# One decode step of attention and a gated feed-forward: larger K, V and query-weight tiles, queries up front, V by pairs of rows, feed-forward over four quadrants

## The chip, the cores and the metric

The kernel runs on 1 core of one Trainium2 chip. The metric is the device time of one execution in microseconds; three runs of the kernel before gave 1093.95, 1096.56 and 1097.2 us.

## The reference

A single token `x` (640 numbers) passes through attention over a cache of 8192 keys and values in each of 32 heads of 192, and then through a gated feed-forward of width 1536. Everything is float32.

```
xn = layernorm(x)
q = xn @ wq                              # wq: 640 x 6144 = 32 heads of 192
for each head: p = softmax(q . K / sqrt(192));  o = p @ V      # K, V: 8192 x 192
h = x + concat(o) @ wo                   # wo: 6144 x 640
hn = layernorm(h)
out = h + (relu(hn @ W_gate) * (hn @ W_up)) @ W_down           # 640 x 1536 twice, 1536 x 640
```

K and V are 402.7 MB of the 445.9 MB that have to be read from HBM. Each element is used once.

## The kernel before

**Loads.** Each head's K and V come in four chunks of 2048 positions. A chunk is one DMA into a tile of 128 partitions by 16 positions (`R = 16`, L35): each partition receives one row of 16 x 192 x 4 = 12,288 bytes that lie together in HBM, 1.57 MB in all. The pool `kv` has 12 such tiles (L55). All loads are issued by SyncE (SP) in program order: K of head h+1 and V of head h by turns (L232 to L238); before the first head of a pair the query weights of the next pair (`load_wq`, L77: 5 rows of 1,536 bytes per partition), before the second the pair's output weights (`load_wo`, L82: one row of 7,680 bytes per partition). An SP instruction whose buffer isn't free holds up all loads behind it. The kernel's loads use eight completion semaphores by turns, so that an issue also waits until the load eight places ahead of it has landed.

**Queries.** `project_q` (L137) makes the queries of two heads, spread to all partitions, in five 128x384 matmuls.

**Scores.** For each chunk VectorE multiplies K in place by the query (L146) and sums 10 of the 16 positions (L147); ScalarE sums the other 6 (L149). A softmax over the 64 x 128 scores follows (L155 to L170): a maximum on VectorE, TensorE to bring it to one partition and back, the exponential on ScalarE, TensorE and VectorE for the sum's reciprocal.

**Values.** For each position row TensorE takes one column of `p` as weights and 192 columns of V, and adds into one partition of `po` (L189): 64 matmuls per head, each recorded as two instructions. In the last two heads VectorE weighs half of the rows (L184, L186). Every two heads the output is turned to columns (L200, L202) and multiplied by the output weights into `acc` (L209), one partition and two banks.

**The last pair and the feed-forward.** The output weights of heads 30 and 31 are loaded as two tiles of 96 partitions (L228) in the two buffers of the tag `wo_t`; the second is issued between loads of V of head 30 and K of head 31. The layer norm of h works on one partition (L297 to L316). The feed-forward takes blocks of 512 columns (rows of 2,048 bytes; `W_down` in rows of 2,560 bytes), and VectorE weighs most slices (L332, L375), TensorE the others, all on one output partition.

Of the kernel before, what the change touches and what calls it, by code (L numbers as in the profile page):

```python
# [15 lines left out]
def kernel(  # L16
# [62 lines left out]

    def load_wo(g):  # L80
        t = wts.tile([P, GJ, D], F32, name="wo_t")
        nc.sync.dma_start(t, wo[g * GW:(g + 1) * GW, :].rearrange("(p j) n -> p j n", p=P))  # L82
        return t

    def load_kv(src, h, c, parts=1):
        t = kv.tile([P, R, DH], F32, name="kv_t")
        v = src[h, c * P * R:(c + 1) * P * R, :].rearrange("(p r) d -> p r d", p=P)
        n = R // parts
        for i in range(parts):
            nc.sync.dma_start(t[:, i * n:(i + 1) * n, :], v[:, i * n:(i + 1) * n, :])  # L90
# [38 lines left out]
    halves = [slice(0, DHALF), slice(DHALF, D)]
    acc = [ps_a.tile([1, DHALF], F32, name=f"acc{i}") for i in range(2)]  # L130
    for i in range(2):
        nc.tensor.matmul(acc[i], ones[0:1, 0:1], xrow[:, halves[i]], start=True, stop=False)

    def project_q(wq_t):
        q = ps_q.tile([P, GW], F32, name="q")
        for j in range(DJ):
            nc.tensor.matmul(q, xn[:, j:j + 1].to_broadcast([P, P]), wq_t[:, j, :],  # L137
                             start=(j == 0), stop=(j == DJ - 1))
        return q

    def scores_of(q, h, kts):
        sc = small.tile([P, NS], F32, name="sc")
        hh = h % GRP
        qb = q[:, hh * DH:(hh + 1) * DH]
        for c, kt in enumerate(kts):
            nc.vector.tensor_mul(kt, kt, qb[:, None, :].to_broadcast([P, R, DH]))  # L146
            nc.vector.reduce_sum(sc[:, c * R:(c + 1) * R - NA], kt[:, :R - NA, :], axis=AX.X)  # L147
# [4 lines left out]

    def softmax_of(sc):
# [16 lines left out]
        nc.vector.reciprocal(rl, pl[0:1, 0:1])  # L170
# [2 lines left out]
    def values_of(p, rl, vts, o, shared):
        """o = p @ V / l; with shared, VectorE weighs and adds some of the rows."""
        po = ps_o.tile([1, DH], F32, name="po")
        va = {}
        for c, vt in enumerate(vts):
            for r in range(R):
                i = c * R + r
                if shared and r % 2:  # L180
                    a = (r // 2) % 2
                    if a not in va:
                        va[a] = row.tile([P, DH], F32, name=f"va{a}")
                        nc.vector.tensor_scalar_mul(va[a], vt[:, r, :], p[:, i:i + 1])  # L184
                    else:
                        nc.vector.scalar_tensor_tensor(va[a], vt[:, r, :], p[:, i:i + 1], va[a],  # L186
                                                       op0=ALU.mult, op1=ALU.add)
                else:
                    nc.tensor.matmul(po, p[:, i:i + 1], vt[:, r, :], start=(i == 0),  # L189
                                     stop=(i == NS - 1))  # L190
        for a in va:
            nc.tensor.matmul(po, ones[:, 0:1], va[a], start=False, stop=(a == len(va) - 1))
        nc.scalar.activation(o, po, AF.Copy, scale=rl)  # L193

    def to_columns(src, n, np_, name):
        """src [1, n * np_] as columns [np_, n]; the row's element is p * n + j."""
        pt = ps_s.tile([P, 512], F32, name="ps_small")
        v = src.rearrange("o (p j) -> o p j", j=n)
        for j in range(n):
            nc.tensor.matmul(pt[0:np_, j:j + 1], v[:, :, j], ones[0:1, 0:1], start=True, stop=True)  # L200
# [1 line left out]
        nc.vector.tensor_copy(t, pt[0:np_, 0:n])  # L202
        return t

    def output_of(o, wo_t, n, np_, last):
        oT = to_columns(o, n, np_, "oT")
        for i in range(2):
            for j in range(n):
                mm = nc.tensor.matmul(acc[i], oT[:, j:j + 1], wo_t[:, j, halves[i]],  # L209
                                      start=False, stop=(last and j == n - 1))  # L210
# [224 lines left out]
```

## Time and profile before

| | |
|---|---|
| runs, us | 1093.95, 1096.56, 1097.2 (median 1096.56) |
| span of the profiled execution, us | 1093.9 |
| instructions | 12264 |
| busy: TensorE, its weight loads | 912.3 us (83%), 427.0 us (39%) |
| busy: VectorE, ScalarE | 767.2 us (70%), 322.4 us (29%) |
| granted TensorE clock, mean | 0.930 |
| read from HBM | 445.91 MB, 408 GB/s over the span |

The profiled execution's span is the lowest of the three times to within 0.1 us. In the profile's lines `128x3072 f32<-...` is output and input as partitions x elements; `x128` counts instructions, then come busy microseconds, mean nanoseconds of one, and idle time before them with what ended it. `SPq` and `ACTq` are the issue streams of SP and ScalarE, `PEld` the weight loads of TensorE.

### The profile page before, as it was taken

To read this page: it belongs to the slowest core of one execution; us is meant where nothing else is said; L and a number is where in the kernel's file an instruction comes from. 1 tells how busy PE (TensorE), PEld (TensorE's weight loads), DVE (VectorE), ACT (ScalarE), POOL (GpSimd) and SP (SyncE) were. 2 spreads that over 40 slices of the span, in tenths; PEclk is the share of its full clock that TensorE was granted. 3 is DMA by queue.
4 is the path that set the end of the run, shared out by engine and by line. 5 is a ranking of instruction groups with operands and counts; after the bars stand their busy time and mean duration, and the time that the engine had idled before them with its cause. 6 is when DMAs were issued, how large, how long until landed. Compare 5 with 4: busy or idle time off the path is not lost.

```text
span 1093.9 us, 12264 instructions
## 1 busy us (share of the span) xinstructions
PE 912.3 (83%) x4698; PEld 427.0 (39%) x4699; DVE 767.2 (70%) x487; ACT 322.4 (29%) x1683; POOL 1.2 (0%) x7
## 2 busy tenths in 40 slices
PE   4599888797988979788897979789797888977598
PEld 2244444343434434343443434334343433433242
DVE  5877767776676776767687766768667677764956
ACT  2423323323222332223232322323223223231220
POOL 0000000000000000000000000000000000000000
PEclk7799999998989989899998999999999999988799
DMA  9999999999999999999999999999999999996994
GB/s 373 425 427 418 425 421 424 420 424 425 422 424 420 425 421 425 425 421 424 420 425 420 424 425 420 425 419 425 422 422 425 421 423 421 425 406 211 414 396 154
DMA packets 55629, 446.70 MB, mean 408 GB/s; under 512 B 4946, under 2 KB 15186, under 8 KB 22932
## 3 DMA queue, kind: packets, MB, share of 16 engines
q1 hardware_dynamic: 55426, 445.93, 98.1%
q8 instruction: 36, 0.59, 0.2%
q14 instruction: 21, 0.17, 0.0%
q10 hardware_dynamic: 146, 0.01, 0.0%
HBM read 445.91 MB, written 0.00 MB: 408 GB/s over the span
## 4 chain that ended last, share of the span: by engine, by line
DMA 74%; PE 11%; DVE 7%; SPq 5%; ACT 2%; issue 1%; ACTq 0%; DVEq 0%
DMA kv_t<-in_A_v_cache_dram 36%; DMA kv_t<-in_A_k_cache_dram 33%; PE po L189 7%; SPq L90 5%; DVE kv_t L146 4%; DMA wq_t<-in_A_wq_dram 3%; DMA wo_t<-in_A_wo_dram 3%; DVE sc L147 1%; ACT kv_t L149 1%; PE acc L209 1%; PE prq L343 1%; PE q L137 1%; DVE va L186 0%; DVE da L375 0%; PE prq L344 0%
## 5 line engine op out<-in xcount | busy, mean ns | idle before, releaser
L189 PE MATMUL po<-kv_t,p 128*1 128x192 f32 x3968 | 716.2, 344 | 129.0 <-DMA kv_t<-in_A_v_cache_dram 129.0
L189 PEld LDWEIGHTS po<-kv_t,p 128*1 128x1 f32 x3968 | 340.2, 88 | 501.9 <-DMA kv_t<-in_A_v_cache_dram 157.3
L146 DVE TENSOR_TENSOR kv_t<-kv_t,q 128x3072 f32<-128x3072 f32 x128 | 428.7, 3350 | 115.8 <-DMA kv_t<-in_A_k_cache_dram 108.7
L149 ACT ACTIVATE kv_t<-kv_t 128x192 f32<-128x192 f32 x768 | 267.6, 349 | 569.4 <-DVE kv_t L146 569.4
L147 DVE TENSOR_REDUCE sc<-kv_t 128x10 f32<-128x1920 f32 x128 | 275.5, 2153 | 3.8
L149 ACT ACTIVATION_READ_ACCUMULATOR kv_t<-kv_t 128x1 f32 x768 | 143.4, 187 | 0.0
L159 DVE TENSOR_REDUCE m<-ps_small 1x1 f32<-1x128 f32 x32 | 8.9, 278 | 124.7 <-PE ps_small L157 124.7
L137 PE MATMUL q<-wq_t,xn 128*128 128x384 f32 x160 | 71.0, 552 | 10.6 <-DMA wq_t<-in_A_wq_dram 10.0
L193 ACT ACTIVATE o<-po,rl 1x192 f32<-1x192 f32 x32 | 13.2, 412 | 143.0 <-PE po L189 127.3
L209 PE MATMUL acc<-wo_t,oT 128*1 128x320 f32 x180 | 52.5, 443 | 0.3 <-DVE oT L202 0.3
L137 PEld LDWEIGHTS q<-wq_t,xn 128*128 128x128 f32 x160 | 28.2, 205 | 28.8 <-issue 12.2
L170 DVE RECIPROCAL rl<-ps_small 1x1 f32<-1x1 f32 x32 | 4.9, 153 | 37.6 <-PE ps_small L168 37.6
L209 PEld LDWEIGHTS acc<-wo_t,oT 128*1 128x1 f32 x180 | 14.1, 85 | 37.2 <-issue 29.2
L186 DVE SCALAR_TENSOR_TENSOR va<-kv_t,p,va 128x192 f32<-128x192 f32 x60 | 20.2, 409 | 0.5 <-DMA kv_t<-in_A_v_cache_dram 0.5
L200 PE MATMUL ps_small<-ones,o 1*128 1x1 f32 (+1 forms) x98 | 19.1, 305 | 0.5 <-ACT o L193 0.5
L161 PE MATMUL ps_small<-m,ones 1*128 1x1 f32 x64 | 12.3, 259 | 8.1 <-DVE m L159 8.1
L200 PEld LDWEIGHTS ps_small<-ones,o 1*128 1x128 f32 (+1 forms) x98 | 17.6, 247 | 1.4 <-ACT o L193 0.9
L168 PE MATMUL ps_small<-ones,rs 128*1 128x1 f32 x64 | 6.0, 164 | 14.5 <-ACT p L166 14.5
L161 PEld LDWEIGHTS ps_small<-m,ones 1*128 1x128 f32 x64 | 9.6, 186 | 19.3 <-DVE m L159 19.3
L202 DVE COPY oT<-ps_small 128x3 f32<-128x3 f32 (+1 forms) x17 | 2.7, 160 | 19.0 <-PE ps_small L200 19.0
L157 PE MATMUL ps_small<-ident,mp 128*1 128x128 f32 x32 | 8.7, 273 | 8.7 <-DVE mp L155 8.7
L168 PEld LDWEIGHTS ps_small<-ones,rs 128*1 128x1 f32 x64 | 2.7, 81 | 23.6 <-ACT p L166 16.0
(86 smaller groups left out, 125.4 us busy)
## 6 DMA issues: line engine op xcount, KB each, us to landing
kv_t<-in_A_k_cache_dram SPq DMA_DIRECT2D x128, 1536.0 KB, 28.1
kv_t<-in_A_v_cache_dram SPq DMA_DIRECT2D x127, 1536.0 KB, 28.1
wq_t<-in_A_wq_dram SPq DMA_DIRECT2D x16, 960.0 KB, 28.4
wo_t<-in_A_wo_dram SPq DMA_DIRECT2D x15, 960.0 KB, 28.4
gu_t<-in_B_W_gate_dram SPq DMA_DIRECT2D x3, 1280.0 KB, 20.7
gu_t<-in_B_W_up_dram SPq DMA_DIRECT2D x3, 1280.0 KB, 25.3
d_t<-in_B_W_down_dram SPq DMA_DIRECT2D x2, 1280.0 KB, 15.9
kv_t<-in_A_v_cache_dram SPq DMA_DIRECT2D x2, 768.0 KB, 26.0
```

What stands on the lines that cost most here:

```text
L90: nc.sync.dma_start(t[:, i * n:(i + 1) * n, :], v[:, i * n:(i + 1) * n, :])
L137: nc.tensor.matmul(q, xn[:, j:j + 1].to_broadcast([P, P]), wq_t[:, j, :], start=(j == 0), stop=(j == DJ - 1))
L146: nc.vector.tensor_mul(kt, kt, qb[:, None, :].to_broadcast([P, R, DH]))
L147: nc.vector.reduce_sum(sc[:, c * R:(c + 1) * R - NA], kt[:, :R - NA, :], axis=AX.X)
L149: nc.scalar.activation(kt[:, r, :], kt[:, r, :], AF.Copy, accum_out=sc[:, c * R + r:c * R + r + 1])
L161: nc.tensor.matmul(pb[:, 0:1], ones[0:1, :], m1, start=True, stop=True)
L186: nc.vector.scalar_tensor_tensor(va[a], vt[:, r, :], p[:, i:i + 1], va[a], op0=ALU.mult, op1=ALU.add)
L189: nc.tensor.matmul(po, p[:, i:i + 1], vt[:, r, :], start=(i == 0), stop=(i == NS - 1))
L193: nc.scalar.activation(o, po, AF.Copy, scale=rl)
L200: nc.tensor.matmul(pt[0:np_, j:j + 1], v[:, :, j], ones[0:1, 0:1], start=True, stop=True)
L209: mm = nc.tensor.matmul(acc[i], oT[:, j:j + 1], wo_t[:, j, halves[i]], start=False, stop=(last and j == n - 1))
L343: nc.tensor.matmul(pr, hT[:, j:j + 1], t[:, j, :], start=(j == 0), stop=False)
```

## The change

- **Tiles.** `R = 32`: K and V come in two chunks per head, each partition receives 24,576 bytes in one row, and the pool `kv` has 6 tiles. The scores still take 16 positions at a time (`SUB`).
- **Queries.** All query weights are loaded first, as five such tiles in the pool `kv`; 60 matmuls of 512 columns, spread over four column groups of TensorE (output partitions 0, 32, 64, 96, called quadrants below), make all queries, 8 heads to a quadrant. `query(h)` spreads one head's query to all partitions by a matmul with a 0/1 matrix `sel`.
- **Values.** Two columns of `p` are the weights and two rows of V (384 columns) the moving side: the wanted sums lie in the two diagonal blocks of a 2 x 384 output. The 32 matmuls of a head go to the four quadrants by turns. `to_columns` picks the diagonal blocks with the 0/1 matrix `par`, and VectorE transposes 32x32 blocks.
- **Output weights.** Four heads share one tile of 15,360 bytes per partition; heads 28 and 29, and 30 and 31, share one of 7,680 bytes. All have 128 partitions. `acc` has a quarter of the 640 columns in each quadrant.
- **Feed-forward.** Weights are taken in whole rows (24,576, 12,288, 6,144 bytes per partition; `W_down` 7,680), TensorE does all products over the quadrants, VectorE none; the layer norm's statistics are over all partitions, and its scale is applied behind the product. The fillers that kept TensorE's clock up (L287) are gone.

The program is ordered by a scheduler, so the diff doesn't show what stands in front of what. SP in the kernel before, at the loads of V of head 30 and K of head 31 (`kv_t` with numbers are K and V tiles, `wo_l0` and `wo_l1` the last two tiles of output weights, `DMAHW` a landing of an earlier load):

```order
L90 DMA kv_t_4495<-in_A_k_cache_dram 128x3072 [waits DMAHW0_49,DVE_49,Activation_49]
L228 DMA wo_l1_4489<-in_A_wo_dram 96x1280 [waits DMAHW1_49,PE_49]
L90 DMA kv_t_4497<-in_A_v_cache_dram 128x3072 [waits DMAHW2_49]
L90 DMA kv_t_4499<-in_A_k_cache_dram 128x3072 [waits DMAHW3_49,DVE_49,Activation_49]
L90 DMA kv_t_4501<-in_A_v_cache_dram 128x3072 [waits DMAHW4_49]
```

The same place in the changed kernel, with the loads that follow up to the feed-forward's first (`wo_t_3428` is the output weights of heads 30 and 31):

```order
L82 DMA kv_t_3322<-in_A_v_cache_dram 128x6144 [waits DMAHW2_49,DMAHW0_49,PE_49]
L90 DMA wo_t_3428<-in_A_wo_dram 128x1920
L82 DMA kv_t_3431<-in_A_k_cache_dram 128x6144 [waits DMAHW3_49,DVE_49,Activation_49]
L82 DMA kv_t_3433<-in_A_v_cache_dram 128x6144 [waits DMAHW4_49,PE_49]
L82 DMA kv_t_3435<-in_A_k_cache_dram 128x6144 [waits DMAHW5_49,DVE_49,Activation_49]
L82 DMA kv_t_3437<-in_A_v_cache_dram 128x6144 [waits DMAHW6_49,PE_49]
L82 DMA kv_t_3543<-in_A_v_cache_dram 128x6144 [waits DMAHW7_49,DVE_49,Activation_49]
L82 DMA kv_t_3545<-in_A_v_cache_dram 128x1536 [waits DMAHW0_49,PE_49]
L283 DMA up_a_3604<-in_B_W_up_dram 128x6144 [waits DMAHW3_49,DVE_49,Activation_49]
L284 DMA rest_3607<-in_B_W_up_dram 128x1536 [waits DMAHW4_49,PE_49]
```

The second output-weight load no longer waits for TensorE, and the one load that is left there waits for nothing. The feed-forward's loads wait for K and V of heads 31 and 30.

TensorE in a middle head of the kernel before, softmax and then values (`p_896` the weights of one head, `po` its output):

```order
L157 MATMUL ps_small_888<-ident_82,mp_886 1x128 [waits DVE_49]
L161 MATMUL ps_small_892<-m1_890,ones_87 128x1 [waits DVE_49]
L168 MATMUL ps_small_899<-ones_87,rs_897 1x1 [waits Activation_49]
L189 MATMUL po_927<-kv_t_907,p_896 1x192 [waits DMAHW6_49]
L189 MATMUL po_927<-kv_t_907,p_896 1x192 x15
L189 MATMUL po_927<-kv_t_911,p_896 1x192 [waits DMAHW0_49]
```

The same in the changed kernel (`q_808` is the query of the head three after that of `p_566`, into the buffer of the head one after it; `mp_654` the next softmax's maximum):

```order
L200 MATMUL ps_small_569<-rs_567,ones_99 128x1 [waits Activation_49]
L232 MATMUL ps_small_573<-ob_521,par_114 32x192 x2
L217 MATMUL po1_221<-kv_t_579,p_566 2x384 [waits DMAHW7_49]
L217 MATMUL po1_221<-kv_t_579,p_566 2x384 x15
L168 MATMUL q_808<-q4_216,sel_108 128x192 [waits DVE_49]
L217 MATMUL po1_221<-kv_t_583,p_566 2x384 [waits DMAHW1_49]
L217 MATMUL po1_221<-kv_t_583,p_566 2x384 x15
L189 MATMUL ps_small_656<-ident_103,mp_654 1x128 [waits DVE_49]
```

A query now stands between the two halves of a head's values, and waits until VectorE has multiplied all of the next head's K; the second half of the values and the next softmax stand behind it. VectorE stands there in the changed kernel as follows (`q_487` is the query of that next head, `sc_523` its scores):

```order
L187 TENSOR_REDUCE mp_458<-sc_425 128x1 [waits DVE_49,Activation_49]
L191 TENSOR_REDUCE m1_462<-ps_small_460 1x1 [waits PE_49]
L202 RECIPROCAL rl_473<-ps_small_471 128x1 [waits PE_49]
L235 STREAM_TRANSPOSE oT_282<-ps_small_475 32x192 [waits PE_49]
L178 TENSOR_TENSOR kv_t_479<-kv_t_479,q_487 128x3072 [waits DMAHW2_49]
L178 TENSOR_TENSOR kv_t_479<-kv_t_479,q_487 128x3072
L179 TENSOR_REDUCE sc_523<-kv_t_479 128x10 [waits DVE_49] x2
```

The next head's scores start only behind the whole softmax and the transpose of the output before it.

The diff, cut to what the prediction speaks of:

```diff
-    R = 16
+    R = 32
...
-    kv = ctx.enter_context(tc.tile_pool(name="kv", bufs=12))
+    kv = ctx.enter_context(tc.tile_pool(name="kv", bufs=6))
...
+    for j in range(DJ):
+        t = kv.tile([P, TW], F32, name="kv_t")
+        nc.sync.dma_start(t, wq_v[:, j, :])
+        wq_ts.append(t)
...
+    for j in range(DJ):
+        for b in range(NQB):
+            for g in range(NQ):
+                c0 = g * HPQ * DH + b * QB
+                nc.tensor.matmul(qps[b][g * Q:(g + 1) * Q, :], xn[:, j:j + 1].to_broadcast([P, Q]),
+                                 wq_ts[j][:, c0:c0 + QB], start=(j == 0), stop=(j == DJ - 1))
...
+    def query(h):
+        g, i = divmod(h, HPQ)
+        q = ps_q.tile([P, QB], F32, tag="q", name="q")
+        nc.tensor.matmul(q[:, 0:DH], sel[:, g, :], q4[:, i * DH:(i + 1) * DH], start=True, stop=True)
+        return q[:, 0:DH]
...
+            for r0 in range(0, R, SUB):
+                ks = k3[:, r0:r0 + SUB, :]
+                nc.vector.tensor_mul(ks, ks, q[:, None, :].to_broadcast([P, SUB, DH]))
+                nc.vector.reduce_sum(sc[:, i0:i0 + SUB - NA], ks[:, :SUB - NA, :], axis=AX.X)
...
+        for i in range(NP):
+            c, r = divmod(2 * i, R)
+            g = i % NQ
+            nc.tensor.matmul(po[g * Q:g * Q + 2, :], p[:, 2 * i:2 * i + 2],
+                             vts[c][:, r * DH:(r + 2) * DH], start=(i < NQ), stop=(i >= NP - NQ))
...
+                nc.tensor.matmul(pt[q0:q0 + Q, 0:W], par[:, k, :], ob[:, k * DH + u * W:k * DH + (u + 1) * W],
+                                 start=(k == 0), stop=(k == 1))
+        nc.vector.transpose(oT[s], pt[s, 0:W].rearrange("p (c j) -> p j c", c=Q))
...
+            for g in range(NQ):
+                nc.tensor.matmul(acc[g * Q:(g + 1) * Q, :], oT[s, j, :], wo_t[s, j, g * DG:(g + 1) * DG],
+                                 start=False, stop=(last and j == J - 1))
...
-                t = wts.tile([WP, WJ, D], F32, tag="wo_t", name=f"wo_l{i}")
-                nc.sync.dma_start(t, wo[r0:r0 + DH, :].rearrange("(p j) n -> p j n", p=WP))
...
+    nc.sync.dma_start(up_a, rows_of(w_up)[:, 0:JA, :])
+    nc.sync.dma_start(up_b, rows_of(w_up)[:, JA, :])
+    nc.sync.dma_start(gt_a[:, 0:2, :], rows_of(w_gate)[:, 0:2, :])
+    nc.sync.dma_start(gt_a[:, 2:4, :], rows_of(w_gate)[:, 2:4, :])
+    nc.sync.dma_start(gt_b, rows_of(w_gate)[:, JA, :])
+    nc.sync.dma_start(dn_b, rows_of(w_down)[:, 0:3, :])
+    for j in range(3, FJ, 3):
+        nc.sync.dma_start(dn_c[:, j - 3:j, :], rows_of(w_down)[:, j:j + 3, :])
...
+            for g in range(NQ):
+                nc.tensor.matmul(ps[g * Q:(g + 1) * Q, 0:FG], hc[:, j, :], w[:, g * FG:(g + 1) * FG],
+                                 start=(j == 0), stop=(j == DJ - 1))
...
+        for g in range(NQ):
+            nc.tensor.matmul(pd[g * Q:(g + 1) * Q, 0:DG], guT[:, j, :], w[:, g * DG:(g + 1) * DG],
+                             start=(j == 0), stop=(j == FJ - 1))
+    nc.vector.scalar_tensor_tensor(o4, pd[:, 0:DG], hr, h4, op0=ALU.mult, op1=ALU.add)
+    for g in range(NQ):
+        (nc.sync if g % 2 else nc.scalar).dma_start(ov[g:g + 1, :], o4[g * Q:g * Q + 1, :])
```

More of the change, by code (lines that the diff above doesn't have):

```diff
@@ new lines, in load_kv, with load_wo @@
+    def load_kv(src, h, c, parts=1):
+        t = kv.tile([P, TW], F32, name="kv_t")
+        v = src[h, c * P * R:(c + 1) * P * R, :].rearrange("(p r) d -> p (r d)", p=P)
+        n = TW // parts
+        for i in range(parts):
+            nc.sync.dma_start(t[:, i * n:(i + 1) * n], v[:, i * n:(i + 1) * n])
+        return t
+    def load_wo(gi):
+        hs = GROUPS[gi]
+        j = len(hs) * DH // P
+        t = wts.tile([P, j, D], F32, tag="wo_t", name="wo_t")
+        r0 = hs[0] * DH
+        nc.sync.dma_start(t, wo[r0:r0 + len(hs) * DH, :].rearrange("(p j) n -> p j n", p=P))
+        return t
@@ L123 @@
     rstd = const.tile([P, 1], F32, name="rstd")
-    rstd_of(rstd, var, P)
+    rstd_of(rstd, var, "x")
     xn = const.tile([P, DJ], F32, name="xn")
     nc.vector.tensor_scalar_mul(xn, xc, rstd)
[L129 to L139, printed above, removed]
@@ L167, in softmax_of @@
         pl = ps_s.tile([P, 512], F32, name="ps_small")
-        nc.tensor.matmul(pl[0:1, 0:1], rs, ones[:, 0:1], start=True, stop=True)
-        rl = small.tile([1, 1], F32, name="rl")
-        nc.vector.reciprocal(rl, pl[0:1, 0:1])
+        nc.tensor.matmul(pl[:, 0:1], ones, rs, start=True, stop=True)
+        rl = small.tile([P, 1], F32, name="rl")
+        nc.vector.reciprocal(rl, pl[:, 0:1])
         return p, rl
[L173 to L193, printed above, removed]
@@ L405 @@
-    nc.vector.tensor_copy(orow[:, halves[0]], dacc[0])
-    nc.scalar.copy(orow[:, halves[1]], dacc[1])
-    nc.sync.dma_start(out[0], orow)
+        gi, i = group_of[h]
+        hs = GROUPS[gi]
+        if i == 0:
+            wo_t = load_wo(gi)
+            oT = small.tile([P, len(hs) * DH // P, Q], F32, tag="oT", name="oT")
+        vts, kts = [], []
+        for c in range(NCH):
+            if h + 1 < H:
+                kts.append(load_kv(kf, h + 1, c))
+            vts.append(load_kv(vf, h, c, 4 if h == H - 1 and c == NCH - 1 else 1))
@@ new lines @@
+    hs1 = row.tile([P, 1], F32, name="hs1")
+    nc.scalar.activation(h4, acc, AF.Copy, accum_out=hs1)
+    hm = ps_s.tile([P, 512], F32, name="ps_small")
+    nc.tensor.matmul(hm[:, 0:1], ones, hs1, start=True, stop=True)
+    hT = row.tile([P, DJ, Q], F32, name="hT")
+    nc.vector.transpose(hT, h4.rearrange("p (c j) -> p j c", c=Q))
+    hmean = row.tile([P, 1], F32, name="hmean")
+    nc.vector.tensor_scalar_mul(hmean, hm[:, 0:1], 1.0 / (D * Q))
+    hc = row.tile([P, DJ, Q], F32, name="hc")
@@ new lines @@
+    pg = ps_q.tile([P, QB], F32, tag="q", name="pg")
+    project(pg, gt_a, gt_b)
+    gu = row.tile([P, FG], F32, name="gu")
+    nc.vector.scalar_tensor_tensor(gu, pg[:, 0:FG], 0.0, us, op0=ALU.max, op1=ALU.mult)
+    guT = row.tile([P, FJ, Q], F32, name="guT")
+    nc.vector.transpose(guT, gu.rearrange("p (c j) -> p j c", c=Q))
+    pd = ps_x.tile([P, QB], F32, tag="x", name="pd")
+    for j in range(FJ):
+        w = dn_b[:, j, :] if j < 3 else dn_c[:, j - 3, :]
+        for g in range(NQ):
+            nc.tensor.matmul(pd[g * Q:(g + 1) * Q, 0:DG], guT[:, j, :], w[:, g * DG:(g + 1) * DG],
+                             start=(j == 0), stop=(j == FJ - 1))
@@ L410 @@
+    o4 = row.tile([P, DG], F32, name="o4")
+    nc.vector.scalar_tensor_tensor(o4, pd[:, 0:DG], hr, h4, op0=ALU.mult, op1=ALU.add)
+    ov = out[0].rearrange("o (g n) -> (o g) n", g=NQ)
+    for g in range(NQ):
+        (nc.sync if g % 2 else nc.scalar).dma_start(ov[g:g + 1, :], o4[g * Q:g * Q + 1, :])
 _INS = ['A_x', 'A_k_cache', 'A_v_cache', 'A_wq', 'A_wo', 'B_W_gate', 'B_W_up', 'B_W_down']
```

335 lines of the change are left out of this document (110 added, 225 removed).

## The prediction

> **What bounds the kernel now.** I read the page first: which engine is full, and in which slices it isn't.
>
> ```profile
> span 1093.9 us, 12264 instructions
> DMA  9999999999999999999999999999999999996994
> GB/s 373 425 427 418 425 421 424 420 424 425 422 424 420 425 421 425 425 421 424 420 425 420 424 425 420 425 419 425 422 422 425 421 423 421 425 406 211 414 396 154
> q1 hardware_dynamic: 55426, 445.93, 98.1%
> HBM read 445.91 MB, written 0.00 MB: 408 GB/s over the span
> ```
>
> The DMA engines are full in every slice but slice 37 and the last. So the time is the bytes over the rate, plus the stretches in which nothing flows; TensorE's 83% and VectorE's 70% lie beside it. Then SP's timeline for the rate. An issue is let go by the landing of the load eight places ahead, so that the distance of two issues is that of two landings. (A K or V tile is 1536 KB; the output weights, 960 KB, were issued just ahead of these rows, and release the last.)
>
> ```profile
> 742.08 0.33 SPq L90 DMA_DIRECT2D kv_t<-in_A_k_cache_dram  x1
> ...
> 764.22 0.33 SPq L90 DMA_DIRECT2D kv_t<-in_A_k_cache_dram  x1
> 766.53 0.33 SPq L90 DMA_DIRECT2D kv_t<-in_A_v_cache_dram  x1
> ```
>
> ```profile
> 92.91 0.33 SPq L82 DMA_DIRECT2D wo_t<-in_A_wo_dram  x1
> 931.75 0.33 SPq L82 DMA_DIRECT2D wo_t<-in_A_wo_dram  x1
> ```
>
> Six K and V tiles take 22.14 us, 3.69 us each: 426 GB/s. The output weights (rows of 7,680 bytes) take 2.31 us: 426 GB/s as well. Between the two lower rows lie 13 pairs of heads, 64.53 us each; 16 x 3.69 + 2.31 leave 3.18 us for the 960 KB of query weights in rows of 1,536 bytes. At the others' rate they would take 2.31, so that 16 of them lose 13.9 us. Last the stretches of the end, by windows (the last three columns are granted TensorE clock, DMA share and GB/s):
>
> ```profile
> 2.00:5.00 3.00, 1.17 (x4) 0.58 (x4) 0.87 (x5) 1.24 (x1) 0.00 (x0) 1.00 0.93 256
> 20.00:27.35 7.35, 3.58 (x6) 2.07 (x7) 7.35 (x3) 3.67 (x21) 0.00 (x0) 0.50 1.02 405
> 980.00:985.00 5.00, 1.63 (x11) 0.68 (x10) 4.57 (x2) 2.19 (x12) 0.00 (x0) 1.00 1.03 322
> 985.00:988.00 3.00, 3.00 (x21) 1.51 (x18) 0.00 (x0) 0.00 (x0) 0.00 (x0) 1.00 1.01 346
> 988.00:990.00 2.00, 1.46 (x9) 0.59 (x7) 1.77 (x1) 0.00 (x0) 0.00 (x0) 1.00 1.06 282
> 990.00:1000.00 10.00, 6.00 (x22) 2.50 (x23) 3.96 (x3) 2.18 (x12) 0.00 (x0) 0.66 0.86 318
> 1000.00:1010.00 10.00, 8.64 (x35) 3.62 (x34) 5.47 (x5) 2.63 (x13) 0.00 (x0) 0.83 0.18 73
> 1010.00:1013.00 3.00, 2.83 (x17) 1.26 (x15) 3.00 (x10) 0.57 (x4) 0.00 (x0) 1.00 0.58 161
> 1013.00:1020.00 7.00, 1.04 (x4) 0.46 (x5) 6.45 (x6) 2.18 (x12) 0.00 (x0) 0.73 1.00 398
> 1076.00:1078.00 2.00, 1.16 (x9) 0.94 (x8) 1.64 (x3) 0.00 (x0) 0.00 (x0) 1.00 0.65 248
> ```
>
> ```profile
> SPq L228 <- PE acc L209: 31.2, 1, 31.2
> ```
>
> From 980 to 1020 the rows' shortfall against 426 sums to 15.6 us (the largest, 10 us at 73 GB/s, is 8.3). Its cause is the one row of SP's waits: the last output weights waited 31.2 us for a buffer that TensorE still read, with all later loads behind them. Full share at 322 to 346 GB/s just before says that the 96-partition load ahead of it also ran badly. After 1077.3 (the last row: 1.3 us' worth of bytes) no data flows, and the span ends 16.6 us later.
>
> **The change, term by term, against the span of 1093.9.**
>
> *Query weights and output weights.* All query weights now have long rows, and the 96-partition loads and the wait at L228 are gone: -13.9 and -15.6 us. What could come next there is the feed-forward's loads, which wait for buffers of heads 30 and 31. K of head 31 has landed two tiles or more before V of head 31 ends, its scores take 10.9 us per tile (below), and a tile takes 7.3 us to load: the buffers are free about 10 us before the stream gets to them. Cost nothing; if that cover failed, up to 15 us as now.
>
> *Feed-forward weights* are 11.8 MB and came in rows of 2,048 and 2,560 bytes:
>
> ```profile
> DMA packets 1376, 3.15 MB, mean 393 GB/s; under 512 B 45, under 2 KB 45, under 8 KB 1376
> ```
>
> (this is 1068 to 1076 us, `W_down` and the last blocks). 30.0 us become 27.7: -2.3.
>
> *Rows of 24,576 bytes.* No row of the trace shows any. By the two rates, one of 16 engines takes 104 ns for 2,560 bytes (2560 x 16 / 393) and 461 ns for 12,288 (3.69 us / 8): 36.7 ps per byte and 10 ns per row. Carried on, 24,576 bytes take 912 ns and a tile 7.30 us; if 12,288 is already on the flat part, 7.38. The difference, 0.08 us for 132 tiles, is 10.6 us. I take the line, since its two ends are a factor of five apart and the new size only two beyond them; the other is the range's, and a rival. The Trainium skill ("DMA: Bandwidth & Descriptors", Measured) has 425 GB/s for a load of 16 MB, which speaks for the flat part; by it the result is that rival's.
>
> *After the last byte.* Of the products only those of the last `W_down` load (12 matmuls of 160 columns) then remain.
>
> ```profile
> 1086.61 3.39 PE L370 MATMUL po<-d_t,guT 128*1 128x320 f32 x12
> 1091.88 0.32 SPq L407 DMA_DIRECT2D out_dram<-orow  x1
> ```
>
> Six matmuls of 320 columns took 3.39 us, so 160 columns take 0.28: 0.9 us four at a time, 3.4 in turn. About 2 us for the last engines' data (the fade after 1076), 1.5 for these, 0.5 for one VectorE operation, and 2.4 for the store (2.0 from its issue to the end now, 0.4 for a second issue on each queue): 6.4 instead of 16.6, -10.2 us.
>
> *The sum, made directly.* 3.2 us until data flows (2.0, and 1.2 short in the first window row); 132 tiles of 7.30; V's last tile in four parts of 6,144 bytes (236 ns by the line) 7.5; output weights 7 x 4.6 + 2 x 2.3 = 36.8; feed-forward 27.7; the program's own fetch 1.3 (estimate: it now is 0.2% of the span and there are fewer instructions); 6.4 behind. That is 1046.5. Subtracting instead, 1093.9 - 13.9 - 15.6 - 2.3 - 10.2 - 10.6 gives 1041.3. I take 1045.3, nearer the direct sum. The median of the runs lies 2.7 above the profiled span: 1048.
>
> *What must hold beside it.* VectorE and TensorE now form a loop per head.
>
> ```profile
> L146 DVE TENSOR_TENSOR kv_t<-kv_t,q 128x3072 f32<-128x3072 f32 x128 | 428.7, 3350 | 115.8 <-DMA kv_t<-in_A_k_cache_dram 108.7
> L147 DVE TENSOR_REDUCE sc<-kv_t 128x10 f32<-128x1920 f32 x128 | 275.5, 2153 | 3.8
> ...
> ```
>
> ```profile
> 1038.79 0.21 DVE L155 TENSOR_REDUCE mp<-sc 128x1 f32<-128x64 f32 x1
> 1041.32 0.15 DVE L170 RECIPROCAL rl<-ps_small 1x1 f32<-1x1 f32 x1
> 1044.45 9.91 PE L189 MATMUL po<-kv_t,p 128*1 128x192 f32 x60
> ```
>
> ```profile
> L202 DVE COPY oT<-ps_small 128x3 f32<-128x3 f32 x15 | 2.4, 161 | 14.7 <-PE ps_small L200 14.7
> L405 DVE COPY orow<-po 1x320 f32<-1x320 f32 x1 | 0.5, 478 | 0.8 <-PE po L403 0.8
> ```
>
> ```profile
> 23.77 6.46 PE L137 MATMUL q<-wq_t,xn 128*128 128x384 f32 x10 [10.04 <-DMA wq_t<-in_A_wq_dram]
> ```
>
> Scores: 4 x (3.35 + 2.15) = 22.0 us per head, the last two reductions (4.3) behind the last multiply. Softmax: 2.7 us now from the maximum to the reciprocal; with the sum over 128 outputs, two 192-column matmuls (0.33 each) and a transpose of 192 columns (0.16 to 0.48 by the copies L202 and L405, not seen here as such) 3.8. Between last multiply and softmax stand the new query (0.8) and half a head's values, P. Loop: 22.0 + 3.8 + max(0, 0.8 + P - 4.3). The stream gives a head 4 x 7.30 + 4.6/4 = 30.4 us.
>
> P is 16 matmuls of 384 columns. 30 matmuls of 192 took 9.91 us, so one of 384 takes 0.66: P is 2.6 if four quadrants run at once, 10.6 in turn. With P = 2.6 the loop is 25.8, hidden. But TensorE will idle most of each head, and the row of 23.77 shows what follows: 1.29 us for 384 columns, at a granted clock of 0.50 in its window. Then P is 5.2, TensorE's other parts double (softmax 5.3, query 1.6), and the loop is 22.0 + 5.3 + 2.5 = 29.8: still hidden, by 0.6 us. Were it 1 us longer, 32 heads would fall up to 13 us behind: within the range below. The Trainium skill ("TensorE: Matmul & The Clock Gate", Part 1) has the clock halved after some 3.4 us without work; the trace agrees (0.50), and it is the rule against this change, though by it alone the sum stays.
>
> **The rivals.** *Rows no faster* (flat): 1048 + 10.6 = 1059. For it: 7,680 and 12,288 bytes already look alike, 426 GB/s. Against: a fixed part per row explains 393 and 426 with one line.
>
> *Quadrants in turn* (slower). No matmul of before uses a quadrant other than the first, so the profile is silent. P = 10.6 makes the loop 22.0 + 3.8 + 7.1 = 32.9, VectorE and TensorE the bound; it decides above P = 8.1, and is slower than before from about 9.7 (1.5 us more per head). The 60 query matmuls (0.88 us each for 512 columns) end at 3.2 + 7.3 + 53 = 63.5, scores begin near 66; 32 heads of 32.9 end at 1119, and values of head 31 (21), products of output, up, gate, down (3.4 + 26.4 + 13.4 us at 0.66 and 0.28), and 12 us of norm, gating and store make about 1195. The Trainium skill ("TensorEngine Tiling (Array Packing)", Key Properties) says that tiles of the array work independently and can run at the same time, which no run here shows.
>
> *A new stall at a seam* (first head, or feed-forward loads), as large as the one removed: 1064.
>
> *Longer rows run worse*: full share at 322 GB/s shows that a load's shape can cost a quarter. Slower than before if the stream falls below 412 GB/s; at 393 the 446 MB take 1135 and the time is about 1148.
>
> **How the numbers follow.** Forecast 0.56, flat rows 0.20, seam 0.08; quadrants in turn 0.11, bad rows 0.05. The first three are faster: 0.84. The slower two: 0.16, of which I leave 0.01 for something that cancels to within 0.3%, about what a measurement of this kernel can tell from no change. The range leaves the slower two out: from 1040 (the subtracted sum) to 1070 (seam, with some of the flat rows).
>
> **What would show it.** Right: DMA share at nine in all slices up to the last, no SP wait behind L228's place, K and V issues 7.3 us apart, TensorE's L217 rows in bursts of 3 to 6 us at a clock near half, and data until some 6 us from the end. Wrong: VectorE's scores following one another without a wait for DMA (quadrants in turn), a low GB/s slice (seam), or 7.4 us and more per tile (flat or bad rows).

## The result and the profile after

The changed kernel takes 1055.54 us (median of four runs, 1055.0 to 1055.73) against 1096.65 for the kernel before beside it: a ratio of 0.9636, 95% interval 0.9621 to 0.9651. The forecast was 1048 within 1040 to 1070. The profiled execution's span is 1053.9 us where 1045.3 was forecast; the median lies 1.6 above it. From the page of the changed kernel:

```profile
span 1053.9 us, 8860 instructions
PE 439.4 (42%) x3136; PEld 135.6 (13%) x3136; DVE 727.0 (69%) x418; ACT 325.1 (31%) x1676; POOL 1.9 (0%) x11
...
DMA  9999999999999999999999999999999999999995
GB/s 391 431 428 432 433 430 430 427 431 428 430 431 430 430 430 428 431 429 431 429 430 430 432 431 429 428 428 430 431 429 433 430 428 427 435 428 429 431 418 231
...
q8 instruction: 24, 0.39, 0.2%
q14 instruction: 20, 0.16, 0.0%
```

DMA is full in every slice but the last, at about 430 GB/s instead of 423; TensorE's busy time has halved. VectorE's timeline around one head (start, duration, what it waited for), with two such rows from the start and the end of the heads:

```profile
112.06 6.62 DVE L178 TENSOR_TENSOR kv_t<-kv_t,q 128x3072 f32<-128x3072 f32 x2 [0.40 <-DMA kv_t<-in_A_k_cache_dram]
...
478.53 6.62 DVE L178 TENSOR_TENSOR kv_t<-kv_t,q 128x3072 f32<-128x3072 f32 x2 [3.83 <-DMA kv_t<-in_A_k_cache_dram]
...
494.11 6.62 DVE L178 TENSOR_TENSOR kv_t<-kv_t,q 128x3072 f32<-128x3072 f32 x2
...
508.44 6.62 DVE L178 TENSOR_TENSOR kv_t<-kv_t,q 128x3072 f32<-128x3072 f32 x2 [3.58 <-DMA kv_t<-in_A_k_cache_dram]
...
519.28 0.22 DVE L187 TENSOR_REDUCE mp<-sc 128x1 f32<-128x64 f32 x1
521.35 0.28 DVE L191 TENSOR_REDUCE m<-ps_small 1x1 f32<-1x128 f32 x1 [1.85 <-PE ps_small L189]
...
524.39 6.62 DVE L178 TENSOR_TENSOR kv_t<-kv_t,q 128x3072 f32<-128x3072 f32 x2
...
537.66 6.62 DVE L178 TENSOR_TENSOR kv_t<-kv_t,q 128x3072 f32<-128x3072 f32 x2 [2.53 <-DMA kv_t<-in_A_k_cache_dram]
...
999.13 6.62 DVE L178 TENSOR_TENSOR kv_t<-kv_t,q 128x3072 f32<-128x3072 f32 x2 [4.54 <-DMA kv_t<-in_A_k_cache_dram]
```

VectorE waits for each head's second K tile, so the starts that carry a wait are landings. From 508.44 to 537.66 are 29.22 us for four tiles, 7.305 each (forecast 7.30). From 478.53 to 508.44 are 29.91: now and then a tile is 0.69 us late. The 29 heads from 112.06 to 999.13 take 887.07 us; at 29.22 a head, with six loads of output weights of 4.6 and two of 2.34, they would take 879.7. So 7.4 us are lateness of that kind. VectorE's own loop is 30.28 (494.11 to 524.39) less 3.58 of waiting, 26.7 us.

The end of the stream, by windows (duration; busy time of five engines; granted clock, DMA share, GB/s):

```profile
1030.00:1040.00 10.00, 7.28 (x72) 2.15 (x68) 0.00 (x0) 0.58 (x1) 0.00 (x0) 0.86 0.97 403
...
1042.00:1044.00 2.00, 1.21 (x24) 0.68 (x24) 0.23 (x1) 0.00 (x0) 0.00 (x0) 0.74 0.49 196
...
1046.00:1048.00 2.00, 1.49 (x24) 0.97 (x24) 0.00 (x0) 0.00 (x0) 0.00 (x0) 0.50 0.06 23
1048.00:1050.00 2.00, 1.50 (x28) 0.73 (x23) 0.00 (x0) 0.00 (x0) 0.00 (x0) 0.50 0.02 8
```

A share of 0.06 is one of 16 DMA engines. Some engines are done near 1040, others at 1044, and one alone works on until 1048.6 (a share of 0.02 over 2 us is 0.6 us of one engine): each part of `W_down` waits for it, and the span ends 5.3 us after it.

### The profile page after: what moved, and what is told of

Same layout as the page of the kernel before. It is cut to its first block, busy times and chain, and to the rows that moved or that the text cites. A ratio compares the mean times of both kernels' runs of the same rounds, so it can differ in the third digit from the quotient of the medians.

```text
span 1053.9 us, 8860 instructions
## 1 busy us (share of the span) xinstructions
PE 439.4 (42%) x3136; PEld 135.6 (13%) x3136; DVE 727.0 (69%) x418; ACT 325.1 (31%) x1676; POOL 1.9 (0%) x11
## 4 chain that ended last, share of the span: by engine, by line
DMA 62%; DVE 28%; PE 8%; issue 1%; ACT 1%; SPq 0%; DVEq 0%
DMA kv_t<-in_A_k_cache_dram 57%; DVE kv_t L178 19%; DVE sc L179 7%; PE po L217 5%; DMA up_a<-in_B_W_up_dram 3%; DMA dn_a<-in_B_W_down_dram 2%; PE q L168 1%; PE ps_small L232 1%; ACT p L198 0%; PE ps_small L193 0%; PE ps_small L200 0%; DVE oT L235 0%; DVE m L191 0%; SPq L74 0%; PE ps_small L189 0%
## 5 line engine op out<-in xcount | busy, mean ns | idle before, releaser
L178 DVE TENSOR_TENSOR kv_t<-kv_t,q 128x3072 f32<-128x3072 f32 x128 | 423.3, 3347 | 165.7 <-DMA kv_t<-in_A_k_cache_dram 165.1
L217 PE MATMUL po<-kv_t,p 128*2 128x384 f32 x2048 | 296.7, 749 | 249.1 <-DMA kv_t<-in_A_v_cache_dram 249.1
L168 PE MATMUL q<-q,sel 128*128 128x192 f32 x64 | 31.0, 589 | 285.6 <-DVE kv_t L178 285.6
L217 PEld LDWEIGHTS po<-kv_t,p 128*2 128x2 f32 x2048 | 60.5, 111 | 453.0 <-DMA kv_t<-in_A_v_cache_dram 274.6
L168 PEld LDWEIGHTS q<-q,sel 128*128 128x128 f32 x64 | 15.6, 303 | 316.5 <-DVE kv_t L178 242.2
L220 ACT ACTIVATE ob<-po,rl 128x384 f32<-128x384 f32 x32 | 18.6, 580 | 111.8 <-PE po L217 111.8
L191 DVE TENSOR_REDUCE m<-ps_small 1x1 f32<-1x128 f32 x32 | 8.9, 279 | 40.5 <-PE ps_small L189 40.5
L232 PE MATMUL ps_small<-ob,par 128*32 128x192 f32 (+1 forms) x144 | 25.6, 314 | 0.7 <-ACT ob L220 0.7
L159 PE MATMUL qp<-kv_t,xn 128*32 128x512 f32 x120 | 21.0, 862 | 11.1 <-DMA kv_t<-in_A_wq_dram 10.1
L200 PE MATMUL ps_small<-rs,ones 128*128 128x1 f32 x64 | 12.4, 264 | 24.9 <-ACT p L198 24.9
L241 PE MATMUL acc<-wo_t,oT 128*32 128x160 f32 (+1 forms) x408 | 18.2, 330 | 4.6 <-DVE oT L235 4.6
L241 PEld LDWEIGHTS acc<-wo_t,oT 128*32 128x32 f32 (+1 forms) x408 | 13.2, 119 | 9.3 <-DVE oT L235 7.8
## 6 DMA issues: line engine op xcount, KB each, us to landing
kv_t<-in_A_wq_dram SPq DMA_DIRECT2D x5, 3072.0 KB, 13.9
```

The lines of the kernel that those rows point to most:

```text
L159: nc.tensor.matmul(qps[b][g * Q:(g + 1) * Q, :], xn[:, j:j + 1].to_broadcast([P, Q]), wq_ts[j][:, c0:c0 + QB], start=(j == 0), stop=(j == ...
L168: nc.tensor.matmul(q[:, 0:DH], sel[:, g, :], q4[:, i * DH:(i + 1) * DH], start=True, stop=True)
L178: nc.vector.tensor_mul(ks, ks, q[:, None, :].to_broadcast([P, SUB, DH]))
L200: nc.tensor.matmul(pl[:, 0:1], ones, rs, start=True, stop=True)
L217: nc.tensor.matmul(po[g * Q:g * Q + 2, :], p[:, 2 * i:2 * i + 2], vts[c][:, r * DH:(r + 2) * DH], start=(i < NQ), stop=(i >= NP - NQ))
L220: nc.scalar.activation(ob, po, AF.Copy, scale=rl)
```

## The experiments

The changed kernel is the base unless said. Ratios are to the kernel before, run beside each; its median ranged from 1094.55 to 1096.65 us. Differences in us are to the base's 1055.54, which was measured at another time, so that one of 2 us is not clear of noise by itself.

**Shorter rows.** The tile as two halves along the partition's row, each from its own half of the chunk:

```
-        v = src[h, c * P * R:(c + 1) * P * R, :].rearrange("(p r) d -> p (r d)", p=P)
+        T = 2
+        v = src[h, c * P * R:(c + 1) * P * R, :].rearrange("(t p r) d -> p t (r d)", t=T, p=P)
...
+        tt = t.rearrange("p (t n) -> p t n", t=T)
...
+            nc.sync.dma_start(tt, v)
```

> The changed kernel with K and V tiles as two rows of 12,288 bytes per partition instead of one of 24,576 (same bytes, same number of loads, other positions on each partition). Theory (a fixed 10 ns per row, from the line through 2,560 and 12,288 bytes): 8 rows more per engine and tile, 0.08 us x 127 tiles = +10.2 us on the changed kernel's 1055.5, about 1065.7, and K landings 29.8 us apart instead of 29.2. Rival (12,288 bytes are already on the flat part): no change, 1055.5.

1064.93 us, ratio 0.9719 (0.9705 to 0.9734): +9.4, where the line said 10.2. Two landings of this run are 29.51 apart, 0.29 more than 29.22 (four times 0.08 is 0.32; the 29.8 of the expectation was misworked).

```profile
512.75 6.62 DVE L189 TENSOR_TENSOR kv_t<-kv_t,q 128x3072 f32<-128x3072 f32 x2 [3.70 <-DMA kv_t<-in_A_k_cache_dram]
542.26 3.35 DVE L189 TENSOR_TENSOR kv_t<-kv_t,q 128x3072 f32<-128x3072 f32 x1 [2.77 <-DMA kv_t<-in_A_k_cache_dram]
```

The fixed cost per row holds between 12,288 and 24,576 bytes; the flat rival falls. The trace's packet records (one for each row that an engine moves) say the same: the median row of 12,288 bytes takes 0.462 us, one of 24,576 bytes 0.914, 10 ns less than two.

**Short rows for the query weights alone** (`ts` and `vs` are the tile and the weights in blocks of 384 columns, each load takes every fourth block):

```
-        nc.sync.dma_start(t, wq_v[:, j, :])
+        for b in range(4):
+            nc.sync.dma_start(ts[:, b], vs[:, b])
```

> The changed kernel with its five query-weight tiles in rows of 1,536 bytes again, as four loads each. Theory A, the prediction's subtraction (16 loads of such rows lost 13.9 us): +13.9, about 1069.4. Theory B, the line of 10 ns per row and 36.7 ps per byte (66 ns for 1,536 bytes, 128 rows per engine and tile): 8.5 instead of 7.3 us per tile, +6 us, about 1061.5, so that more than half of the 13.9 was something else in those pairs, such as fetches of the program.

1060.89 us, ratio 0.9683 (0.9667 to 0.9699): +5.4, theory B. Less than half of the 13.9 us was the rows.

**Twice the TensorE program.**

```
+    def pads(mm, n):
+        with tc.issue_after(mm.ins):
+            for _ in range(n):
+                nc.tensor.matmul(pad[:, 0:1], padw, padw[:, 0:1], start=True, stop=True)
```

> The changed kernel with 96 bf16 matmuls of one column per head beside the work (64 after the first half of the values, 32 after the head's transpose; their result is used nowhere): 6,144 more TensorE instructions, which doubles its program, 24 more fetches of 16 KB. Theory (a fetch falls on one of 16 DMA engines, and a tile lands with its slowest engine): +7 to +9 us, about 1063.5, with some of the K landings 0.4 to 0.7 us late. Rival 1 (the bytes are spread evenly): 0.39 MB at 424 GB/s, +0.9 us, 1056.5. Rival 2 (the added matmuls lengthen the loop of VectorE and TensorE): VectorE would no longer wait for DMA before each head's scores.

1055.28 us, ratio 0.9634 (0.9619 to 0.9648): no difference to the base, and the theory fell in this form. The page shows the fetches, and the windows of the end show where they went:

```profile
q8 instruction: 48, 0.79, 0.3%
```

```profile
1046.00:1048.00 2.00, 1.21 (x32) 0.68 (x24) 0.00 (x0) 0.00 (x0) 0.00 (x0) 1.00 0.55 216
1048.00:1050.00 2.00, 0.70 (x16) 0.49 (x16) 0.00 (x0) 0.00 (x0) 0.00 (x0) 0.81 0.06 23
```

Some nine engines (a share of 0.55) now work until 1048, where one did; the last ends about when it did. So q8's fetches are spread over engines that had some 4 us to spare, which 24 more fetches have nearly used up, and something else sets the last one. The other program queue, q14, was left.

**More and fewer ScalarE instructions.** First 48 copies of one column per head added:

```
+                nc.scalar.copy(pada, ones[:, 0:1])
```

> The changed kernel with 48 copies of one column on ScalarE per head in ScalarE's idle time (24 behind the first tile's scores, 24 behind the softmax), used nowhere: 1,536 more ScalarE instructions, 12 more fetches of 8 KB on queue q14. After the doubled TensorE program cost nothing, the theory is: q8's fetches (TensorE) go round several DMA engines, q14's fall on one, which is the one that trails by some 7 us at the end of the stream, and each costs it the 0.69 us by which a head's last K tile lands late now and then: 12 x 0.69 = +8.3 us, about 1064. Rival (program fetches of any engine cost nothing; another thing makes one DMA engine trail): 1055.5.

1065.02 us, ratio 0.972 (0.9705 to 0.9734): +9.5 for 12 fetches, 0.79 each.

```profile
q14 instruction: 32, 0.26, 0.1%
```

```profile
1045.00:1050.00 5.00, 3.30 (x36) 0.69 (x28) 0.00 (x0) 0.33 (x1) 0.00 (x0) 1.00 0.07 29
...
1056.00:1058.00 2.00, 1.02 (x24) 0.68 (x24) 0.00 (x0) 0.00 (x0) 0.00 (x0) 0.95 0.06 23
```

One engine now trails from 1045 until 1058, and the engines that compute don't hold it up (VectorE waits 170.2 us for K in all, 165.1 in the base). Then fewer instructions, by giving VectorE more of the sums:

```
-    NA = 6
+    NA = 4
```

> The changed kernel with 4 instead of 6 of each 16 score rows reduced by ScalarE (NA = 4), the other 12 by VectorE: 512 ScalarE instructions fewer, 4 fetches of 8 KB fewer. Theory (q14's fetches fall on one DMA engine at 0.69 us each): -2.8 us, about 1052.7. Against: VectorE gets 1.7 us more per head, of some 5 us that it waits for DMA. Rival 1 (fetches cost nothing): 1055.5. Rival 2 (VectorE's loop comes to the fore): later than 1055.5, and VectorE's wait for DMA gone.

1052.57 us, ratio 0.9606 (0.9592 to 0.962): -3.0 for four fetches.

```profile
q14 instruction: 16, 0.13, 0.0%
```

And with `NA = 3`:

> The changed kernel with 3 instead of 6 of each 16 score rows reduced by ScalarE: 768 ScalarE instructions fewer, 6 fetches of 8 KB fewer than the changed kernel and 2 fewer than with 4 rows. Theory (0.69 us per fetch on the one DMA engine that trails): -4.1 us against the changed kernel, about 1051.4, and 1.1 us below the version with 4 rows. Rivals: the nine engines that end next (some 4 us ahead of the last in the changed kernel) decide now: 1051 to 1052; VectorE, with 2.6 us more per head, becomes the bound: above 1053.

1051.48 us, ratio 0.9592 (0.957 to 0.9615): -4.1 for six.

```profile
q14 instruction: 14, 0.11, 0.0%
```

The three together give 0.68 to 0.79 us per fetch of 8 KB. With 4 rows the lone engine ends at 1046:

```profile
1044.00:1046.00 2.00, 1.49 (x24) 0.90 (x24) 0.00 (x0) 0.00 (x0) 0.00 (x0) 0.72 0.07 27
1046.00:1048.00 2.00, 1.02 (x24) 0.68 (x24) 0.38 (x1) 0.00 (x0) 0.00 (x0) 1.00 0.00 0
```

With 3 it ends soon after 1044, nearly level with the next ones:

```profile
1042.00:1044.00 2.00, 1.41 (x24) 0.99 (x24) 0.00 (x0) 0.00 (x0) 0.00 (x0) 0.59 0.48 192
1044.00:1046.00 2.00, 1.50 (x26) 0.81 (x22) 0.00 (x0) 0.00 (x0) 0.00 (x0) 0.50 0.02 8
```

VectorE still waits 106.3 us for K in all. This version has the lowest median of all that were tried, below both kernels.

The base's own trace ties the late landings to these fetches. This is what its queues carried between the landings at 478.53 and 508.44, where one is late:

```profile
q8 instruction: 1, 0.02, 0.2%
q14 instruction: 1, 0.01, 0.1%
```

and between 449.32 and 478.53 (29.21 us), where none is:

```profile
q8 instruction: 1, 0.02, 0.2%
```

From 292.63 to 999.13 there are 23 such stretches. Ten are late, by 0.66 to 0.70 us each, and each of these ten has one or two fetches of q14; of the other thirteen none has one, though eight have one of q8. In the three stretches with two fetches of q14 only one step shows, so not every such fetch delays the landings. The six stretches before are less clear: two are late, by 0.25 and 0.39 us, and only the second has such fetches, while two others that have them are on time. Why one costs 0.69 us stays open: by the row's line 8 KB take one engine 0.31.

**Larger tiles.** K and V in one tile of 48 KB rows, three buffers:

```
-    R = 32
+    R = 64
-    kv = ctx.enter_context(tc.tile_pool(name="kv", bufs=6))
+    kv = ctx.enter_context(tc.tile_pool(name="kv", bufs=3))
```

> The changed kernel with tiles twice as large: K and V in rows of 49,152 bytes, three buffers instead of six, each feed-forward matrix in rows up to 30,720 bytes. Theory (10 ns per row): 8 rows fewer per engine for each 48 KB tile, 0.08 us x 64 = -5 us, about 1050. Rival 1 (flat from 24,576 bytes): 1055.5. Rival 2 (three buffers are too few: a tile's buffer is needed back 27 us after it landed, its scores take 22): every head waits 1 us or more, 1070 or above, with a wait of SP's queue on VectorE in each head that leaves DMA idle.

1053.44 us, ratio 0.9619 (0.9603 to 0.9634): -2.1, between theory and rivals, and not clear of noise: the ratio's interval overlaps the base's, and the four executions run from 1052.77 to 1055.19. The page, of the slowest of them, has slices above 435 GB/s that the base never has, and others, most of them early, below 420:

```profile
GB/s 394 439 433 392 418 416 431 442 426 435 429 432 435 428 435 423 437 437 427 434 431 430 431 417 434 433 428 433 428 423 440 422 427 430 435 428 431 423 422 260
```

The saving per row is there in the trace's packet records (a median of 1.818 us for 49,152 bytes, 10 ns less than two rows of 24,576), but more than half of the 5 us of the theory is missing. That they are lost in the low slices, to loads that come late, is a guess that no run tests. Together with `NA = 4`:

> Tiles of 48 KB in three buffers, and 4 instead of 6 of 16 score rows reduced by ScalarE, the two edits that each gained (2.1 and 3.0 us). Theory (they save different things, time per row and ScalarE's fetches): the sum, 1050.4. Rival (VectorE's 1.7 us more per head releases the three buffers later, and the stream waits): above 1052.6, with a longer wait of SP's queue on VectorE and lower GB/s slices.

1052.61 us, ratio 0.9604 (0.9581 to 0.9628): no gain over `NA = 4` alone. The two don't add. SP waits 819.8 us for VectorE's scores here and 797.5 in the run before, which is the rival's way; which buffer is late was not followed further.

**One quadrant.**

```
-            nc.tensor.matmul(po[g * Q:g * Q + 2, :], p[:, 2 * i:2 * i + 2],
-                             vts[c][:, r * DH:(r + 2) * DH], start=(i < NQ), stop=(i >= NP - NQ))
+            nc.tensor.matmul(po[0:2, :], p[:, 2 * i:2 * i + 2],
+                             vts[c][:, r * DH:(r + 2) * DH], start=(i == 0), stop=(i == NP - 1))
```

> The changed kernel with all value matmuls in the first quadrant, in one group, instead of four at a time. Theory (the quadrants run at once, and it is this that keeps the loop hidden): half a head's 16 matmuls of 384 columns take 0.66 us each at full clock, 10.6 us instead of 5.1; the loop is 22.0 + 3.8 + 7.1 = 32.9 us per head against the stream's 30.4 and decides: 32 heads fall 2 to 2.5 us behind each, about +60 to +80 us less what the buffers still hide, 1115 to 1135; VectorE's scores follow each other without a wait for DMA. Rival (TensorE is hidden either way): 1055.5.

1066.05 us, ratio 0.9726 (0.971 to 0.9742): +10.5, far less than expected. TensorE in this run, 16 matmuls as 32 instructions, against the base's timeline:

```profile
516.29 10.48 PE L217 MATMUL po<-kv_t,p 128*2 128x384 f32 x32
...
1022.78 20.16 PE L217 MATMUL po<-kv_t,p 128*2 128x384 f32 x62
```

```profile
516.05 5.06 PE L217 MATMUL po<-kv_t,p 128*2 128x384 f32 x32
...
1015.73 6.98 PE L217 MATMUL po<-kv_t,p 128*2 128x384 f32 x64
```

The windows of the two upper rows, first in this run, then in the base (granted clock, DMA share and GB/s come last):

```profile
516.29:526.77 10.48, 10.48 (x34) 2.71 (x33) 7.12 (x4) 1.64 (x10) 0.00 (x0) 1.00 1.00 427
```

```profile
516.05:521.11 5.06, 5.06 (x34) 1.07 (x33) 3.35 (x3) 1.22 (x8) 0.00 (x0) 0.54 1.02 437
```

P is 10.48 us at a granted clock of 1.00, and 5.06 over four quadrants at 0.54, which would be 2.7 at 1.00: at one clock the four quadrants are nearly four times as fast, as forecast. Over the whole run TensorE is busy for 80% of the span at a mean clock of 0.917, in the base for 42% at 0.669. The Trainium skill ("TensorEngine Tiling (Array Packing)", Key Properties) says that different tiles of the array can execute matmuls in parallel; the trace agrees (5.06 against 10.48 us). VectorE shows why the loop stays hidden:

```profile
523.14 3.35 DVE L178 TENSOR_TENSOR kv_t<-kv_t,q 128x3072 f32<-128x3072 f32 x1 [2.98 <-DMA kv_t<-in_A_k_cache_dram]
527.01 0.28 DVE L191 TENSOR_REDUCE m<-ps_small 1x1 f32<-1x128 f32 x1 [0.52 <-PE ps_small L189]
```

While TensorE works on the values, VectorE multiplies half of the next head's first tile: here the scheduler put this between the two maxima (L187 and L191), and VectorE even waits for K. The changed kernel has it behind the whole softmax. So this run shows that a P of 10.5 us can be hidden, but not what it would cost in the changed kernel's order. The 10.5 us arise behind the last V, where head 31's values (the lower rows) end at 1043 instead of 1023; half of these 20 us are hidden, since the base waits for `W_down` meanwhile.

**One buffer for the output weights.**

```
-    wts = ctx.enter_context(tc.tile_pool(name="wts", bufs=2))
+    wts = ctx.enter_context(tc.tile_pool(name="wts", bufs=1))
```

> The changed kernel with one buffer instead of two for the output weights, so that a group's load waits for the group before to be multiplied, with all later loads of SP's queue behind it. Theory (such a wait cost 15.6 us of stream in the kernel before; here the queue holds some 40 us of loads issued ahead, and the output weights are used 47 us after their issue): 5 to 11 us in each of the 8 later groups, +40 to +90 us, with dips in the GB/s row at each. Rival (what is issued ahead covers the wait): 0 to +5 us.

1107.64 us, ratio 1.0105 (1.0084 to 1.0126): +52.1, 1% longer than the kernel before. In SP's waits:

```profile
SPq L90 <- PE acc L241: 290.5, 8, 37.9
```

Eight waits of 36 us; 52.1 / 8 is 6.5 us of stream lost at each, so the loads issued ahead covered some 30. So a stall of the kind of L228 costs time where the stream is the bound.

**The stall in the kernel before, alone.**

```
-                t = wts.tile([WP, WJ, D], F32, tag="wo_t", name=f"wo_l{i}")
+                t = (row if i else wts).tile([WP, WJ, D], F32, tag="wo_r" if i else "wo_t", name=f"wo_l{i}")
```

> The kernel before, with a buffer of its own for the second of the two last output-weight loads, so that it waits for nothing (L228's wait on the product at L209 is gone; all else as before). Theory (that wait held all later loads and cost the stream about what the windows from 990 to 1020 lack, 15.6 us with what the 96-partition load lacks): -12 to -15 us, about 1083. Rival (the stall is hidden, or comes back as another wait behind it): 1096.

1099.64 us against 1096.3, ratio 1.0037 (1.0023 to 1.0052): no gain, 0.4% longer, and the theory fell. The windows:

```profile
980.00:985.00 5.00, 1.10 (x6) 0.32 (x5) 4.39 (x2) 2.19 (x12) 0.00 (x0) 0.82 1.04 230
...
990.00:1000.00 10.00, 6.96 (x34) 3.03 (x33) 5.39 (x3) 2.18 (x12) 0.00 (x0) 0.84 1.01 291
...
1060.00:1070.00 10.00, 10.00 (x32) 4.26 (x31) 3.00 (x12) 2.48 (x7) 0.00 (x0) 0.76 0.90 342
1070.00:1080.00 10.00, 9.47 (x26) 2.39 (x25) 7.52 (x12) 2.00 (x5) 0.00 (x0) 0.90 0.05 21
```

The wait is gone, and the stream ends near 1070 instead of 1077. But the span (1098.6) ends 28 us behind it instead of 16.6: TensorE is busy for 19.5 of the 20 us from 1060 on, and its products were what ended last. Why the kernel takes 3 us more than before, and not the same time, stays open. The two 96-partition loads now stand side by side, at full share and 230 to 291 GB/s in the first two rows.

**Loads of 96 partitions** (the other 32 partitions of the tile are set to zero).

```
+            for i in range(2):
+                nc.sync.dma_start(t[0:96, 2 * i:2 * i + 2, :],
+                                  wo[r0 + i * DH:r0 + (i + 1) * DH, :].rearrange("(p j) n -> p j n", p=96))
```

> The changed kernel with the output weights of the last two groups (four heads) loaded as the kernel before loaded its last two: one load per head of 96 partitions with 5,120 bytes each, in place of two loads of 128 partitions with 7,680 bytes (same bytes; the rows stand on other partitions than the product expects, so that the output isn't the reference's). Theory (it was the shape of these loads that slowed the stream at full share: in the kernel before with a buffer of its own, 230 to 301 GB/s from 980 to 1000 us lack 6.9 us against 425 for two of them): four cost +10 to +14 us, about 1067, with slices near 300 GB/s at full share behind 890 and 950 us. Rival (the slow stretch came from something else of that kernel's end, such as its feed-forward): 0 to +1 us, 1056.

1069.32 us, ratio 0.9772 (0.9755 to 0.9788): +13.8, 3.4 us more for each load of 0.49 MB, whose bytes take 1.2 at the others' rate.

```profile
905.00:910.00 5.00, 0.00 (x0) 0.00 (x0) 4.07 (x2) 0.68 (x4) 0.00 (x0) 0.50 0.96 216
910.00:915.00 5.00, 1.01 (x2) 0.50 (x2) 5.00 (x3) 3.69 (x22) 0.00 (x0) 0.50 1.06 241
915.00:920.00 5.00, 1.19 (x8) 0.25 (x12) 1.89 (x2) 0.00 (x0) 0.00 (x0) 0.50 0.97 339
```

The Trainium skill ("SBUF — State Buffer", Door 1: The DMA port swizzle) says that the rate depends on how many of 16 ports the partitions reach. By its table 96 partitions give half of the ports four partitions instead of eight, which as an estimate makes 0.75 of the rate, 323 GB/s. The stream ran worse than that beside these loads, at 216 to 241 GB/s in the first two rows. The packet records of the trace show that it isn't only their own rows: rows of 24,576 bytes took a median of 1.6 to 1.7 us from 905 to 915, and 0.914 in the rest of the run. Why, the run doesn't show.

## Why the prediction was right, and where it was off

- **The bound and the direction**: the stream bounds the kernel, the quadrants run at once, nothing on an engine that computes decides, and no seam stalls (the DMA row is at nine up to the last slice). Right.
- **Rows by the line**: right, 7.305 us per tile. Undone for K and V, it costs 9.4 of the 10.2 that the line gives for their 127 tiles. The time alone wouldn't have shown it: 1055.54 lies nearer the flat rows' 1059 than the forecast's 1048. The landings and the run with shorter rows tell the two apart.
- **Query weights, -13.9**: mis-sized; the rows are worth 5.4. The issues in the kernel before from which the term was worked out show the rest:

```profile
738.33 0.33 SPq L82 DMA_DIRECT2D wo_t<-in_A_wo_dram  x1
802.32 0.33 SPq L82 DMA_DIRECT2D wo_t<-in_A_wo_dram  x1
867.06 0.33 SPq L82 DMA_DIRECT2D wo_t<-in_A_wo_dram  x1
```

The first distance is 63.99 us, the second 64.74. Of the 13 from 92.91 to 931.75, three are 63.99 to 64.02 and ten are 0.3 to 1.0 longer. At 64.00 the query weights of a pair take 2.65 instead of 3.18, and 16 x (2.65 - 2.31) is 5.4, as measured. The other 8.5 us are lateness that only some pairs have, which the mean over 13 pairs put on the query weights. The changed kernel has lateness too, 7.4 us of it. What makes the pairs late in the kernel before wasn't tested.

- **The stall at L228, -15.6**: no term of its own. By the run with 96 partitions, two such loads are 6.9 of it (half of 13.8), and taking away the wait gained nothing in the kernel before, where TensorE's work ended last. With the short tail such a wait costs time (6.5 us each with one buffer). So the cut of TensorE's work at the end and the end of the stall are one gain; that is argued from these two runs, as none has the one stall with the short tail. The subtraction took them for two; the direct sum was the safer way, and still too low.
- **The loop**: P 5.06 for 5.2, at a clock near half as forecast; the softmax with its wait (519.28 to 524.39) 5.1. Of this 1.85 are the wait behind the values, so that the softmax alone is 3.3, not 5.3. The loop is 26.7, not 29.8, and hidden by 3.6 us.
- **Quadrants in turn, 1195**: not tested in the order that it was priced for. Its step "between last multiply and softmax" has VectorE idle during the values, which is the changed kernel's order; the run with P = 10.48 has another, in which VectorE worked on the next tile, and the price there was 10.5 us, at the end.
- **Behind the last byte**: 5.3 us from the last engine's end. The forecast's 6.4 has 4.4 for this, and 2.0 for engines that end later than the others.
- **The program's fetch, 1.3 us**: the term that makes up most of the miss. It was taken as bytes spread over 16 engines. The runs show that q14's fetches make one engine late, by 0.68 to 0.79 us for each fetch added or left out, and that loads end with the slowest engine: 7.4 us up to head 31.

Putting these in the direct sum, 1046.5 - 1.3 - 2.0 + 7.4 + 0.9 (5.3 for 4.4) gives 1051.5, of 1053.9. The 2.4 left can be the lone engine's further lateness behind 999; it wasn't separated. That the miss stayed inside the range is in part luck: its upper end was set for a seam and flat rows, which didn't come, and the 1045.3 was pulled down by a subtraction that counted 8.5 us of lateness as saved.

## What to carry to other kernels

Where DMA is full in every slice, look at the last windows for a share of one sixteenth: what makes one DMA engine late, here the fetches of ScalarE's program, is paid in full, and fetches on engines with time to spare are free until that time is used up. A stall in the stream is worth its length only if the engines behind it would be done in time; try it alone before adding it to other gains. Spread a load over all 128 partitions, and give it long rows: 24,576 bytes paid here against 12,288, while 49,152 in half as many buffers gained nothing clear.
